# Taking GpSimd out of a chunked recurrence: scaling, masks and clearing on VectorE, -v as one product, decoding behind the last solve

## The chip, the cores and the metric

The kernel runs on one core of one Trainium2 chip. The metric is the device time of one execution in microseconds (us). An engine's instructions run in the order in which the program holds them; the five engines and the DMA queue of SyncE (SP) wait for each other through semaphores.

## The reference

Three layers follow each other on float32 data.

```python
# 1: delta rule, B=4, H=8 (32 heads), S=768 tokens, D=48
k_n = k / (norm(k) + 1e-6)
for t in range(S):
    y[:, :, t] = q[t] @ state                      # state: 48x48 per head
    v_old = state^T @ k_n[t]
    state = state + beta[t] * outer(k_n[t], v[t] - v_old)
# 2: soft mixture of 8 experts with 4 slots each over x = y (3072 tokens x 384)
logits = x @ phi                                   # 32 slots
slot_in = softmax over tokens (logits).T @ x
slot_out = relu(slot_in @ w1) @ w2                 # expert by expert, 384 -> 1024 -> 384
x = softmax over slots (logits) @ slot_out
# 3: gated feed-forward, 384 -> 2048 -> 384
h = x @ w_in;  out = (h * sigmoid(1.702 h)) @ w_out
```

`w_in` and `w_out` arrive as float64 and are turned to float32 on the chip by integer operations ("decoding").

## The kernel before

**Recurrence.** The 768 tokens are cut into 24 steps of 32 (`NS`, index i); four steps make a group (`GS`, 6 groups, index gq). Within a step the delta rule is a triangular system of 32x32 per head. For each step `grams` multiplies k with k and k with q; ScalarE copies the results out of PSUM, and the k-q part (`pm`) is masked to its triangle (L491), by GpSimd in steps 16 to 23 (`PMX`) and by VectorE in the others. For each group `solve` inverts the triangular systems of all its steps on VectorE: a transpose (L499), a clearing of the result `xx` by ScalarE (`clear`, L392), norms of k by small steps, 31 elimination steps of a product (L531) and an addition (L535) each, and a transpose back (L539, called `nt`).

A step itself is `chain(i, g)`, for two halves g: V puts -v into a PSUM bank by a product with the negated identity (L571), KS adds k times state onto it (L578), four pieces of 32 partitions are copied out as `rbd` (three by ScalarE, L589, and one by VectorE, L591, which subtracts v itself instead of taking V's help), U multiplies with the inverse (L604), the result is copied to `ubd` (L614), S adds to the state in PSUM (L622), which ScalarE copies out as `sbd` (L633) for the next step, and QS (L598) and Y (L644) give the output. v has been scaled by the norm of k before (`scale_v`, L740, on GpSimd), as soon as its load has landed. `logits` follows with transposes (T, L657) and the running softmax over tokens.

**Order.** All of this up to the dispatch of tokens to slots is not issued as written. `Plan` collects the operations with an engine, a duration from the kernel's own cost function and their dependencies, works out start times by list scheduling and then by passes from the latest times back and forward again, and issues everything in the order of these times. It knows five engines and SP's queue; a weight load counts 4.4 us (`WD`) there, a load of v 0.6 us plus 2.0 until its data can be used, plus 0.28 us from one engine to another. Where it sees TensorE idle for long, `fill` puts in small products on a zero tile (L383), as many as its own times leave room for. `DBONUS` lowers the rank of decoding in the first of these passes.

**Weights.** SP loads four blocks of `w_in` into slots during the recurrence, `win_decode` turns them to float32 on VectorE in 16 pieces of three passes (L242, L243, L244). Blocks of `w1` and `w2` (8 each, 1.5 MB) go to wherever the recurrence leaves room: two slots early, four `wb` buffers, the ring `cs` of the last three steps (`tail_in`), and the slots that decoding frees (L752).

**Behind the plan** everything is written out by hand: the experts (`expert_in`, `hidden_t`, `expert_out`), which load the rest of `w2` and then `w_out` as blocks come free, the products of `w_in` with the slots, and the final loop over 96 blocks, in which VectorE decodes `w_out` and GpSimd splits it (L1040).

## Time and profile before

| what | value |
|---|---|
| median of 3 runs | 529.67 us (528.14 to 534.84) |
| the profiled execution, its own time | 530.09 us |
| its span, first to last instruction | 528.4 us |
| busy: TensorE, VectorE, ScalarE, GpSimd | 496.1, 344.1, 326.9, 70.8 us |
| mean granted TensorE clock | 0.987 of full speed |
| GpSimd: scalings of v; masks | 24, 22.0 us; 8, 6.3 us |
| moved by DMA | 76.45 MB |

Busy times are sums over a profiled execution whose span is a little shorter than its time. Where products run beside each other in different columns of TensorE, its busy time counts the stretch once. A row of a timeline gives start, duration, engine, line, operation, the tile written and those read, how many instructions are merged in it, and in brackets how long the engine was idle before and what released it. A row of groups gives busy time, mean duration and the idle time before.

### The profile page before, as it was taken

How to read it: one execution, taken by the hardware profiler on the slowest of the kernel's cores; microseconds unless marked ns; L12 is line 12 of the kernel's file. 1: busy time of each engine (PE TensorE's matmuls, PEld its weight loads, DVE VectorE, ACT ScalarE, POOL GpSimd, SP SyncE). 2: the span in 40 equal slices, each digit the busy share in tenths (PEclk: the TensorE clock that was granted, in tenths of full speed). 3: DMA queues.
4: the chain of work that ended last, by engine and by line, in shares of the span. 5: the costliest groups of instructions: out<-in, count | busy, mean ns of one | idle time of the engine just before them, and what ended most of it. 6: DMA issues, size and time to landing. Idle time of an engine off the chain costs nothing.

```text
span 528.4 us, 17593 instructions
## 1 busy us (share of the span) xinstructions
PE 496.1 (94%) x7414; PEld 416.8 (79%) x7414; DVE 344.1 (65%) x910; ACT 326.9 (62%) x736; POOL 70.8 (13%) x113
## 2 busy tenths in 40 slices
PE   7679998999989989999899999999999999999997
PEld 6559776667667667667554898899999999999997
DVE  4989899799998998978653699732333333323322
ACT  8492688778888889787331654644544544545442
POOL 5100011121112011420511333200000000000000
PEclk9798999999999999999989999999999999999999
DMA  8776559666786674687999400100100100100101
GB/s 170 202 195 177 122 158 284 165 174 192 277 285 218 229 249 132 212 297 255 386 419 424 195 0 2 60 1 1 60 1 0 62 1 0 61 0 4 57 2 60
DMA packets 27631, 76.45 MB, mean 145 GB/s; under 512 B 3424, under 2 KB 12640, under 8 KB 24608
## 3 DMA queue, kind: packets, MB, share of 16 engines
q1 hardware_dynamic: 27552, 75.33, 43.8%
q8 instruction: 58, 0.95, 0.8%
q14 instruction: 21, 0.17, 0.1%
HBM read 70.60 MB, written 4.72 MB: 143 GB/s over the span
## 4 chain that ended last, share of the span: by engine, by line
PE 67%; ACT 13%; DVE 10%; DMA 4%; issue 4%; SPq 1%; POOL 0%; DVEq 0%; ACTq 0%; POOLq 0%
PE ps_s L1082 13%; PE ps_g L1082 7%; PE ps_y L1082 7%; PE ps_t L1082 6%; PE ps_s L622 5%; PE ps_x L604 4%; ACT rbd L589 3%; DMA wa<-in_kq_dram 3%; PE ps_x L1044 3%; PE ps_y L598 2%; PE ps_y L644 2%; ACT sbd L633 2%; PE ps_t L383 2%; PE ps_s L955 2%; ACT ubd L614 2%
## 5 line engine op out<-in xcount | busy, mean ns | idle before, releaser
L1049 DVE TENSOR_TENSOR glo<-wa,ghi 128x512 fp32r<-128x512 f32 x96 | 66.4, 691 | 125.3 <-ACT wa L1048 125.3
L1082 PE MATMUL ps_s<-wo,ghi 128*128 128x384 f32 x300 | 81.3, 336 | 0.0
L1047 ACT ACTIVATE ghi<-ps_x 128x512 fp32r<-128x512 f32 x64 | 38.3, 598 | 60.1 <-PE ps_x L1044 59.3
L531 DVE TENSOR_TENSOR wb<-wb,wb 128x87 f32<-128x87 f32 (+25 forms) x211 | 70.0, 346 | 2.3
L535 DVE TENSOR_TENSOR wb<-wb,wb 128x87 f32<-128x87 f32 (+25 forms) x211 | 68.4, 338 | 2.3
L1082 PEld LDWEIGHTS ps_s<-wo,ghi 128*128 128x128 f32 x300 | 54.8, 188 | 2.0
L633 ACT COPY sbd<-ps_s 48x384 f32<-48x384 f32 x92 | 43.4, 473 | 11.7 <-PE ps_s L622 10.0
L1082 PE MATMUL ps_g<-wo,ghi 128*128 128x384 f32 x150 | 50.3, 335 | 0.0
L1082 PE MATMUL ps_y<-wo,ghi 128*128 128x384 f32 x150 | 50.3, 335 | 0.0
L589 ACT COPY rbd<-ps_x 32x192 f32<-32x192 f32 x138 | 42.7, 310 | 6.7 <-PE ps_x L578 3.8
L740 POOL TENSOR_TENSOR cs<-cs,nr 128x384 f32<-128x384 f32 x24 | 22.0, 920 | 176.3 <-DMA cs<-in_vt_dram 104.8
L1082 PE MATMUL ps_s<-wo,glo 128*128 128x384 f32 x150 | 40.6, 335 | 0.0
L598 PE MATMUL ps_y<-sbd,cs 112*32 112x96 f32 x736 | 37.4, 251 | 3.1 <-issue 2.7
L1082 PE MATMUL ps_t<-wo,ghi 128*128 128x384 f32 x120 | 40.2, 335 | 0.0
L466 PE MATMUL ps_g<-wa 112*32 112x64 f32 x896 | 32.6, 225 | 7.5 <-issue 5.1
L1047 ACT ACTIVATE ghi<-ps_y 128x512 fp32r<-128x512 f32 x32 | 19.2, 599 | 31.0 <-PE ps_y L1044 30.7
L1048 ACT ACTIVATE wa<-ps_x 128x512 f32<-128x512 f32 x64 | 38.0, 594 | 0.0
L578 PE MATMUL ps_x<-sbd,cs 112*32 112x96 f32 x736 | 32.5, 249 | 0.3 <-ACT sbd L633 0.2
L466 PEld LDWEIGHTS ps_g<-wa 112*32 112x32 f32 x896 | 23.3, 111 | 10.6 <-issue 7.3
L383 PEld LDWEIGHTS <-warm 128*128 128x128 bf16 x520 | 26.4, 105 | 4.5 <-issue 1.7
L1082 PEld LDWEIGHTS ps_y<-wo,ghi 128*128 128x128 f32 x150 | 28.2, 188 | 0.7
L1082 PEld LDWEIGHTS ps_g<-wo,ghi 128*128 128x128 f32 x150 | 28.2, 188 | 0.7
(297 smaller groups left out, 1073.8 us busy)
## 6 DMA issues: line engine op xcount, KB each, us to landing
cs<-in_kq_dram SPq DMA_DIRECT2D x48, 224.0 KB, 3.6
wa<-in_w_dram SPq DMA_DIRECT2D x7, 1536.0 KB, 8.9
wb<-in_w_dram SPq DMA_DIRECT2D x6, 1536.0 KB, 8.6
wa<-in_kq_dram SPq DMA_DIRECT2D x42, 192.0 KB, 4.4
cs<-in_vt_dram SPq DMA_DIRECT2D x24, 192.0 KB, 3.6
cs<-in_w_dram SPq DMA_DIRECT2D x3, 1536.0 KB, 8.7
cs<-in_wout_dram SPq DMA_DIRECT2D x3, 1536.0 KB, 15.2
out_dram<-wa SPq DMA_DIRECT2D x24, 192.0 KB, 1.9
```

The costliest lines, as they stand in the source:

```text
L383: nc.tensor.matmul(ps[bank][:, 416:512], warm, warm[:, 0:96], start=True, stop=True)
L466: nc.tensor.matmul(pg[32 * n : 32 * n + 32, z, 2 * m : 2 * m + 2], kds[a][0:112, 4 * j + c], kqd[a][0:112, z, :, 4 * j + c], start=True, s ...
L531: engs[e].tensor_tensor(tmp, xx[:, lo:top, j : j + 1].to_broadcast([P, n, m]), gu[:, j : j + 1, j + 1 :].to_broadcast([P, n, m]), op=ALU.mult)
L535: engs[e].tensor_tensor(xx[:, lo:top, j + 1 :], xx[:, lo:top, j + 1 :], tmp, op=ALU.add)
L578: nc.tensor.matmul(pr[32 * j : 32 * j + 32, c - 2 * g].rearrange("p h e -> p (h e)"), kci[0:112, 4 * j + c], sbd[0:112, j, c].rearrange("p ...
L589: n = nc.scalar.copy(rbd[q, 2 * g : 2 * g + 2, :, j], pr[q])
L598: nc.tensor.matmul(py[32 * j : 32 * j + 32, c].rearrange("p h e -> p (h e)"), qci[0:112, 4 * j + c], sbd[0:112, j, c].rearrange("p h e -> ...
L633: apart(sbs, e, copy[e](sbn[r, :, 2 * g : 2 * g + 2, h], ps_s[g][r]))
L1047: nc.scalar.activation(ghis[k % 3], phs[k % 3], AF.Gelu_apprx_sigmoid)
L1048: nc.scalar.activation(ggs[k % 3], phs[k % 3], AF.Gelu_apprx_sigmoid)
L1049: nc.vector.tensor_tensor(glos[k % 3], ggs[k % 3], ghis[k % 3], op=ALU.subtract)
L1082: nc.tensor.matmul(po[f][:, 0:DM], l_[:, 128 * f : 128 * f + 128], w_out(fc, r), start=(fc == 0 and l_ is ghi and r == 0), stop=False)
```

## The change

GpSimd's scaling of v, its masks and ScalarE's clearing of `xx` for groups 2 to 5 go to VectorE. -v is one product with the whole negated identity for all four pieces, and VectorE's piece of `rbd` becomes a plain copy. ScalarE's cost function has 0.1 us of fixed part in place of 0.052, and V counts 0.33 in place of 0.054. Steps 18 and 19 have both `ubd` copies of a half on ScalarE. `win_decode` is called at the end, depends on the last solve's transpose, and loses its lowered rank. Of the weights, `w1` blocks 2 and 3 go into the ring of steps 21 and 22, `w2` block 0 into that of step 23, and `w2` blocks 1 and 2 into the slots behind decoding; the tables of who lies where (`w2t`, `rawt`) follow.

```diff
--- before.py
+++ after.py
@@ -34,14 +34,13 @@
 FREE = 12
 NA, NBS = 4, 4
 SPLIT = (((0, "dve", 0, 6), (1, "dve", 6, 32)), ((0, "dve", 0, 32),))
-DBONUS = -10.0
 GH = 32
 PAD = 1.0
-PMX = range(16, 24)
+PMX = ()
 
 COPY = (
     (0, ("dve", "act", "act", "act"), ("act", "act"), ("act", "act")),
-    (18, ("dve", "act", "act", "act"), ("dve", "act"), ("act", "act")),
+    (20, ("dve", "act", "act", "act"), ("dve", "act"), ("act", "act")),
 )
 DP = 384
 FBANK = "t"
@@ -399,7 +398,7 @@
             clear(ubds[n].rearrange("p a b c d -> p (a b c d)"), 1536, [("ubd", n, c) for c in range(4)])
 
     def cost(eng, n):
-        return {"dve": (n + 62) / 960.0, "act": 0.052 + n / 1200.0, "pool": 0.15 + 0.00166 * n, "padd": 0.15 + 0.0021 * n}[eng]
+        return {"dve": (n + 62) / 960.0, "act": 0.1 + n / 1200.0, "pool": 0.15 + 0.00166 * n, "padd": 0.15 + 0.0021 * n}[eng]
 
     def dma(dst, src, key, d=0.6):
         pl.add("sp", d, lambda: nc.sync.dma_start(dst, src), (), key if isinstance(key, list) else [key], after=2.0)
@@ -498,7 +497,10 @@
         gk, xk, mk = ("gu", z), ("xx", z), ("sm", z)
         pl.add("dve", 2.0, lambda: nc.vector.transpose(gu, nt.rearrange("p a c h t -> p t (a c h)")),
                [("gs", gq % 4, st) for st in range(GS)], [gk, (gk, 1)])
-        clear(xx.rearrange("p a b -> p (a b)"), 1024, [xk])
+        if gq < 2:
+            clear(xx.rearrange("p a b -> p (a b)"), 1024, [xk])
+        else:
+            pl.add("dve", 0.6, lambda: nc.vector.memset(xx, 0.0), (), [xk])
         diag = gu.rearrange("p a b -> p (a b)")[:, :: C + 1]
         small = lambda f, rd, wr, d=0.105: pl.add("dve", d, f, rd, wr)
 
@@ -536,7 +538,7 @@
 
                 pl.add(e, cost(e, n * m), f1, [gk if j < GH else (gk, 1), xk, (xk, z_)], [("tmp", z, z_, j % 2)], nm=f"sv{gq}")
                 pl.add(e, cost("padd" if e == "pool" else e, n * m), f2, [("tmp", z, z_, j % 2), xk], [(xk, z_)], nm=f"sv{gq}")
-        pl.add("dve", 2.0, lambda: nc.vector.transpose(nt.rearrange("p a c h t -> p t (a c h)"), xx.rearrange("p s t -> p t s")),
+        pl.first["nt", gq] = pl.add("dve", 2.0, lambda: nc.vector.transpose(nt.rearrange("p a c h t -> p t (a c h)"), xx.rearrange("p s t -> p t s")),
                [(xk, 0), (xk, 1), xk], [("gs", gq % 4, st) for st in range(GS)], nm=f"nt{gq}")
 
     def two(i):
@@ -564,20 +566,16 @@
         pr = px[:, 0:192].rearrange("p (c h e) -> p c h e", c=2, h=2)
 
         zero = i == 0
-        qa = [j for j in range(4) if rq[j] == "act" and not zero]
 
         def f():
-            for j in qa:
-                nc.tensor.matmul(px[32 * j : 32 * j + 32, 0:192], negi[:, 32 * j : 32 * j + 32],
-                                 vs[i % VB][:, 4 * g : 4 * g + 4].rearrange("p a e -> p (a e)"), start=True, stop=False)
-        if qa:
-            pl.add("pe", 0.054, f, [("v", i % VB)], [kx], nm=f"V{g}.{i}", cols=192 * len(qa))
+            nc.tensor.matmul(px[:, 0:192], negi, vs[i % VB][:, 4 * g : 4 * g + 4].rearrange("p a e -> p (a e)"), start=True, stop=False)
+        if not zero:
+            pl.add("pe", 0.33, f, [("v", i % VB)], [kx], nm=f"V{g}.{i}", cols=768)
         for c in cs if not zero else ():
             def f(c=c):
                 for j in range(4):
                     nc.tensor.matmul(pr[32 * j : 32 * j + 32, c - 2 * g].rearrange("p h e -> p (h e)"), kci[0:112, 4 * j + c],
-                                     sbd[0:112, j, c].rearrange("p h e -> p (h e)"), start=j not in qa,
-                                     stop=j not in qa or c == cs[1])
+                                     sbd[0:112, j, c].rearrange("p h e -> p (h e)"), start=False, stop=(c == cs[1]))
             pl.first["KS", i] = pl.add("pe", 0.24, f, [("kc", i % VB)] + ksb, [kx], nm=f"KS{g}.{i}", cols=420)
         made = []
         for j in range(4):
@@ -588,7 +586,7 @@
                 elif rq[j] == "act":
                     n = nc.scalar.copy(rbd[q, 2 * g : 2 * g + 2, :, j], pr[q])
                 else:
-                    n = nc.vector.tensor_tensor(rbd[q, 2 * g : 2 * g + 2, :, j], pr[q], vi[q, 2 * g : 2 * g + 2], op=ALU.subtract)
+                    n = nc.vector.tensor_copy(rbd[q, 2 * g : 2 * g + 2, :, j], pr[q])
                 if not zero:
                     apart(made, rq[j], n)
             pl.add(rq[j], cost(rq[j], 192), f, [("v", i % VB)] + [kx] * (not zero), [("rbd", g, j)], nm=f"R{g}.{i}")
@@ -736,8 +734,8 @@
     def scale_v(i):
         gq, st = divmod(i, GS)
         v_, nr = vs[i % VB], nrs[gq % 4]
-        pl.add("pool", cost("pool", 384),
-               lambda: nc.gpsimd.tensor_tensor(v_, v_, nr[:, 8 * st : 8 * st + 8].unsqueeze(2).to_broadcast([P, 8, D]), op=ALU.mult),
+        pl.add("dve", cost("dve", 384),
+               lambda: nc.vector.tensor_tensor(v_, v_, nr[:, 8 * st : 8 * st + 8].unsqueeze(2).to_broadcast([P, 8, D]), op=ALU.mult),
                [("nr", gq % 4)], [("v", i % VB)], nm=f"vs{i}")
 
     def solves(i):
@@ -767,14 +765,11 @@
             w = wis[n][:, lo : lo + DP].bitcast(U32)
             key, first = ("wa", NA + n // 2), n == 0 and m == 0
             to = dtmp if first else w
-            k0 = len(pl.ops)
             for s_ in range(3):
                 pl.add("dve", (DP * (1 + (s_ > 0)) + 130) / 1920.0, lambda f=decode(nc, to, raw, to)[s_]: f(), [("wa", PW[n])],
-                       [("dt", n, m)] if s_ == 1 or first else [("dt", n, m), key], nm=f"dc{n}")
+                       [("dt", n, m)] if s_ == 1 or first else [("dt", n, m), key], nm=f"dc{n}", deps=[pl.first["nt", NG - 1]])
             if first:
                 pl.add("dve", (DP + 130) / 1920.0, lambda w=w: nc.vector.tensor_copy(w, dtmp), [("dt", n, m)], [key], nm=f"dc{n}")
-            for k in range(k0, len(pl.ops)):
-                pl.bonus[k] = DBONUS
 
     def slots_in():
         for n in range(2, 4):
@@ -782,11 +777,6 @@
         for n in range(2):
             w1t.append(slots[2 + n])
             weight(slots[2 + n], w1[n], ("wa", 2 + n), nm=f"w1{n}")
-        for n in range(2):
-            win_decode(2 + n)
-        for n in range(2):
-            w1t.append(slots[n])
-            weight(slots[n], w1[2 + n], ("wa", n), nm=f"w1{2 + n}")
 
     def tail_in():
 
@@ -796,14 +786,21 @@
             [k for k in pl.wr if k in (("xx", 0), ("gu", 1), (("gu", 1), 1)) or k[0] == ("xx", 0) or k[0:2] == ("tmp", 1)],
             [k for k in pl.wr if k[0] in ("sm", "tmp", ("xx", 1)) or k in ("bu", ("xx", 1))],
         )
+
+        for n in range(4):
+            win_decode(n)
+        for n in range(2):
+            w1t.append(css[(NS - VB + n) % VB])
         for n in range(NBS):
             w1t.append(wbs[n])
             pl.add("sp", WD, lambda n=n: nc.sync.dma_start(wbs[n], w1[4 + n]), (), held[n], nm=f"w1{4 + n}")
 
         for n in range(VB):
             s_ = NS - VB + n
-            pl.add("sp", WD, lambda s_=s_, n=n: nc.sync.dma_start(css[s_ % VB], w2[n]), (),
+            pl.add("sp", WD, lambda s_=s_, n=n: nc.sync.dma_start(css[s_ % VB], w1[2 + n] if n < 2 else w2[0]), (),
                    [(m, s_ % VB) for m in ("kc", "qc", "v", "k")] + [("pm", i) for i in range(NS // 2, NS) if i % VB == s_ % VB], after=2.0, nm=f"wc{n}")
+        for n in range(2):
+            weight(slots[n], w2[1 + n], ("wa", n), nm=f"w2{1 + n}")
 
     def setup_loads():
         pl.add("sp", 0.5, lambda: nc.sync.dma_start(bu_sb, bu), (), ["bu"], after=2.0)
@@ -844,9 +841,6 @@
             grams(n, [pl.first["KS" if i else "U", i]])
         if i in EXTI:
             win_load(EXTI.index(i), [len(pl.ops) - 1])
-        if i == EXTI[-1]:
-            win_decode(0)
-            win_decode(1)
         if i + LEAD < NS:
             solves(i + LEAD)
 
@@ -872,8 +866,8 @@
     tp = tc.alloc_tile_pool(name="tp", bufs=1, reuse_waits="tile")
 
 
-    w2t = [css[(NS - VB + n) % VB] for n in range(VB)] + [w1t[n] for n in W2P]
-    rawt = [raws[1]] + [cras[(NS - VB + n) % VB] for n in range(VB)]
+    w2t = [css[(NS - 1) % VB], slots[0], slots[1]] + [w1t[n] for n in W2P]
+    rawt = [cras[(NS - 2) % VB], cras[(NS - 1) % VB], raws[0], raws[1]]
 
     def raw_in(n):
         w = 768 if n == 0 else 3072
```

## Rows read from the trace of the kernel before

**Rows 1.** Busy time by stage: window, length, each engine (count), clock, DMA, GB/s.
```profile
54.00:218.50 164.50, 152.85 (x3704) 111.42 (x3707) 150.14 (x454) 137.78 (x351) 23.99 (x27) 1.00 0.67 204
...
259.00:297.00 38.00, 35.06 (x486) 21.23 (x478) 18.09 (x48) 12.55 (x28) 5.80 (x7) 0.96 0.99 410
```

**Rows 2.** The chain of waits, 54 to 218.5 us: shares by line; longest pieces.
```profile
by line: PE ps_s L622 13.7%; PE ps_x L604 9.3%; ACT rbd L589 8.9%; ACT sbd L633 7.4%; ACT ubd L614 5.9%; PE ps_y L598 5.8%; issue 5.3%; PE ps_y L644 5.3%; ACT wb L614 4.8%; PE ps_x L578 4.5%; PE ps_x L571 4.3%; DVE wb L531 4.2%; DVE wb L535
697 pieces in order of time: start us, us, what
...
83.56 1.05 ACT wb L392
...
168.57 1.02 DVE wb L531
```

**Rows 3.** Timeline around two scalings: start, us, engine, line, operation, tiles, shape.
```profile
60.47 0.93 DVE L531 TENSOR_TENSOR wb<-wb,wb 128x252 f32<-128x252 f32 x1
...
211.36 0.32 DVE L531 TENSOR_TENSOR wb<-wb,wb 128x156 f32<-128x156 f32 x1
...
211.41 0.96 POOL L740 TENSOR_TENSOR cs<-cs,nr 128x384 f32<-128x384 f32 x1 [5.84 <-DVE wb L535]
...
211.72 0.83 DVE L535 TENSOR_TENSOR wb<-wb,wb 128x156 f32<-128x156 f32 x1
```

**Rows 4.** Groups by line, GpSimd: busy, mean ns, idle before and what ended it.
```profile
L740 POOL TENSOR_TENSOR cs<-cs,nr 128x384 f32<-128x384 f32 x24 | 22.0, 920 | 176.3 <-DMA cs<-in_vt_dram 104.8 <-DVE wb L531 19.6 <-DVE nr L523 19.3
```

**Rows 5.** The instructions that read v's tensor: from issue to landing, 24 loads.
```profile
DMA to landing us min/median/max: 2.5/3.6/8.6
```

**Rows 6.** Groups by line, VectorE, for prices (L591 of 54 to 218.5 us).
```profile
L243 DVE SCALAR_TENSOR_TENSOR we<-wa,we 128x384 uint32<-128x384 uint32 x8 | 4.4, 554 | 0.2
...
L491 DVE TENSOR_TENSOR wa<-wa,mask 128x256 f32<-128x256 f32 x8 | 3.3, 415 | 0.0
...
L349 DVE COPY wa<-zeros 64x512 f32<-64x512 f32 x4 | 2.3, 639 | 0.0
...
L242 DVE TENSOR_SCALAR we<-we 128x384 uint32<-128x384 uint32 x7 | 2.5, 353 | 0.0
...
L591 DVE TENSOR_TENSOR rbd<-ps_x,cs 32x192 f32<-32x192 f32 x38 | 12.9, 341 | 9.1 <-PE ps_x L578 3.4 <-PE ps_g L466 2.7 <-ACT xt L660 1.2
...
L614 DVE COPY ubd<-ps_x 32x384 f32<-32x384 f32 x10 | 5.5, 549 | 4.3 <-PE ps_x L604 4.2
```

**Rows 7.** Groups by line, ScalarE (L392 has four of 1024 behind 50 us).
```profile
L614 ACT COPY ubd<-ps_x 32x384 f32<-32x384 f32 x46 | 21.6, 470 | 9.2 <-PE ps_x L604 6.9 <-issue 1.4 <-ACT xt L660 0.3
...
L392 ACT COPY wb<-zeros 128x1024 f32<-128x1024 f32 (+1 forms) x7 | 7.8, 1108 | 7.0 <-DVE gs L539 7.0
```

**Rows 8.** Timeline of TensorE, 198 to 199.5 us: transposes, then V products.
```profile
198.44 0.55 PE L657 MATMUL ps_t<-ident,x 128*128 128x128 f32 x3
198.92 0.36 PE L571 MATMUL ps_x<-cs,negi 128*32 128x192 f32 x3
...
199.27 0.34 PE L571 MATMUL ps_x<-cs,negi 128*32 128x192 f32 x3
```

**Rows 9.** Fillers (chain), solve 0's transpose, U of step 0; last transpose, first decode.
```profile
44.17 9.80 PE ps_t L383 x228
...
49.82 1.99 DVE L539 STREAM_TRANSPOSE gs<-wb 128x1024 f32<-128x1024 f32 x1
...
53.90 0.84 PE L604 MATMUL ps_x<-rbd,gs 128*32 128x192 f32 x8
...
216.42 2.04 DVE L539 STREAM_TRANSPOSE gs<-wb 128x1024 f32<-128x1024 f32 x1
...
219.34 0.98 DVE L242 TENSOR_SCALAR dtmp<-we 128x384 uint32<-128x384 uint32 x1
```

**Rows 10.** Timeline behind the plan: product of w1 block 3, first decode of w_out.
```profile
264.89 1.84 PE L928 MATMUL ps_y<-wa,sit 128*32 128x256 f32 x24 [2.00 <-DMA wa<-in_w_dram]
...
284.90 0.36 DVE L242 TENSOR_SCALAR wa<-wa 128x384 uint32<-128x384 uint32 x1 [5.98 <-DMA wa<-in_wout_dram]
```

## The prediction

> **What bounds the kernel now.** I read first the busy time by stage, to see where an edit can matter [rows 1]. The recurrence proper, from the first U product at 54 us to the end of the last solve at 218.5, keeps three engines nearly full: of 164.5 us TensorE is busy 152.9, VectorE 150.1, ScalarE 137.8, GpSimd 24.0. VectorE has 14.4 us to spare. From 259 to 297 the DMA engines are at 0.99 of their time and 410 GB/s. Every GpSimd instruction that the change removes lies before 234 us; the final stage keeps its own.
>
> Second, the chain of waits over that stretch [rows 2]. The reader should see that no engine holds it: S, U, Y, KS and QS products alternate with ScalarE's copies, and VectorE's solve (L531) has 4.2%, the V product (L571) 4.3%. Summed over its 697 pieces VectorE has 19.2 us of the chain's 164.5, ScalarE 51.4, TensorE 83.6. One clearing copy on ScalarE stands in it whole, 1.05 us.
>
> Third, VectorE's order of time beside GpSimd's [rows 3, 4]. A solve step of 128x156 takes 0.32 us, and the next one of that shape takes 0.83, because a GpSimd scaling starts inside the step before it. From the one at 60.47 us to the one at 211.72 there are 22 such VectorE instructions, on average 0.46 us longer than their shape takes alone: 22 x 0.46 = 10.1 us of VectorE's busy time is waiting for GpSimd.
>
> Fourth, the two places where a later stage waits: the fillers ahead of step 0 [rows 9] and the expert product that waits for a load [rows 10].
>
> **The change part by part.** The sum is made against the profiled execution: span 528.4 us, 530.09 in all, 0.4 above the median of 529.67. "In the stretch" is 54 to 218.5 us.
>
> *VectorE's balance in the stretch.* Removed: 10.1 us of waiting, since no GpSimd work is left there. Added: 19 of the 24 scalings of v at 0.55 us (the two-input 128x384 row [rows 6]) = +10.5; eight masks at 0.415 = +3.3; four clearings of 1024 elements. No row has a memset of that size on VectorE. A copy of zeros with 512 elements takes 0.64, so 1.28 by doubling; a one-input pass over 384 takes 0.353, so 0.94 by proportion. I take 1.1, between them and next to ScalarE's 1.05 for the same fill [rows 7]: +4.4 (3.8 to 5.1). Removed again: steps 18 and 19 give their four ubd copies back to ScalarE, 4 x 0.55 = -2.2. The rbd piece that becomes a plain copy from PSUM stays near its 0.34: PSUM reads 32x192 elements either way. Balance: -10.1 + 10.5 + 3.3 + 4.4 - 2.2 = +5.9 us on an engine with 14.4 idle, 9.1 of it in front of rbd pieces that wait for KS [rows 6]. It costs +5.9 if the solve sets the pace all along, 0 if the idle time takes it. The chain is the nearer row: 19.2 of VectorE's 150.1 busy us were on it, 13%, so +0.8.
>
> *ScalarE.* Four clearings leave, 4 x 1.05 = -4.2; four ubd copies come, 4 x 0.47 = +1.9 [rows 7]. Net -2.3, and 51.4 of its 137.8 us were on the chain: -0.9 (-4.2 to +1.9). The clearings do not show elsewhere: the solve that reads them comes later on VectorE itself.
>
> *-V as one product.* The three 32-column products per half step run beside each other: two groups of them start at 198.92 and the next V at 199.27, so 0.35 us [rows 8]. Whole-width, two passes of 0.17 remain, plus what a change of shape costs. The transposes, whole-width between narrow products, show that: three of them hold the engine from 198.44 to 198.92, 0.48 us, while inside such a group the starts are 0.11 apart, so about 0.15 goes to the change. That makes 0.49 for 0.35: +0.14 x 46 = +6.4. V's part of the chain, 4.3% of 164.5 = 7.1, is about half of its 38 x 0.35 in the stretch, so I take half: +3.2. Bounds: 0, if V runs while KS waits for sbd, and +6.4. A gain isn't excluded, since 276 issued pieces become 92: -1.0. The Trainium skill, "TensorEngine Tiling (Array Packing)", Key Properties, says that a change of tiling mode drains TensorE; it speaks against this edit, and by it both sides of each V would pay, which makes this term its upper bound; without it the term is nil. The rows of the transposes side with the page.
>
> *Start.* U of step 0 starts at 53.90, but the solve ends at 51.81: between them TensorE still works off 228 fillers, 9.8 us, which the planner counts from its own times [rows 9]. It now sees three scalings more on VectorE ahead of that solve (0.465 us each by the kernel's own cost function), so it may order up to 1.4 us more fillers; on the chip those scalings (1.7) replace as much waiting for GpSimd. Half: +0.7 (0 to 1.4).
>
> *Later decoding.* In the trace the first decode starts at 219.34, after the last solve's transpose ends at 218.46 [rows 9]: the new dependency orders what already was so. Its 48 passes still lie between dispatch's small VectorE steps, so nothing: 0.
>
> *Moved loads.* w1 block 3 was loaded into the slot that decode 3 frees: its product starts at 264.89, after TensorE waited 2.00 us [rows 10]. It and block 2 now go into the rings that steps 21 and 22 leave, where w2 loads stood before; w2 blocks 1 and 2 take the late slots, and are read only in the second half of the expert stage. On SP's queue the waits keep their places: behind the one on decode 3 stand only the expert stage's loads. POOL's constants had a scaling ahead of them and now have none; dispatch is their only reader. That wait goes: -2.0. Next late is the w_out load, for which VectorE then idles 5.98 us; the DMA engines are full up to it, so its landing won't come forward, which bounds the gain between 0 and -2.0.
>
> Sum: +0.8 - 0.9 + 3.2 + 0.7 + 0 - 2.0 = +1.8, so 530.1 + 1.8 = **532 us**. The terms' own ends, added up, are 521 and 544.
>
> **Rivals.** *The lock was what held the pace.* Each GpSimd operation delays not one solve step but also the rbd and ubd copies queued behind it on VectorE, which the chain books under ScalarE and TensorE. For it: a lengthened solve step of 1.02 us is among the chain's longest pieces [rows 2], and the orders of VectorE were written without these waits. Then the 10.1 us leave the path, the added work goes into the 14.4 idle, ScalarE gives its 2.3 and the load its 2.0, V costs nothing: 530.1 - 10.1 - 2.3 - 2.0 + 0.7 = 516. Against it: the added work is longer than the wait removed.
>
> *VectorE now waits for v's load.* On GpSimd the scaling waited for its DMA at no cost: 104.8 us idle for that [rows 4]. On VectorE everything behind it waits too: solve steps, rbd pieces, then U. The planner counts 0.6 + 2.0 + 0.28 = 2.9 us from issue to use; the trace has a median of 3.6 and a worst of 8.6 [rows 5]. A scaling placed just when the planner thinks it lands stalls VectorE 0.7 us, the worst 5.7: 20 x 0.7 + 5.7 = 19.7 at most. It decides when more than half of that is met: +10 over the forecast, 542. Against it: v is loaded more than a step ahead of its use, and a planner that works back from late times with a full VectorE need not place it at the landing.
>
> *It does not do what it says.* If the planner sets the scalings into waits that VectorE has anyway, if V hides, and if the decode was late already, only the load remains: 528, inside the forecast's band.
>
> **How the numbers follow.** About 2%, 10.6 us, is what a measurement of this kernel can tell from no change: 519.1 to 540.3. Forecast, with the third rival in it: 0.58. The first rival: 0.24, and the second: 0.18; each is past 2%. Both are kept that high since every term of the forecast is a small difference of large ones and the planner reorders the whole recurrence. The forecast's own range is 523 to 539. Eight in ten: I reach down to 517 and up to 542, which leaves out about half of the first rival and under half of the second.
>
> **What would show it.** VectorE's solve steps should all keep their lone duration; the page's GpSimd count should fall by 32 instructions. VectorE's busy time in the recurrence should grow by about 6 us. A wait of VectorE for the v load in the list of waits shows the second rival; the interval between last-solve ends, below 32 us, the first. V products should show two pieces per half step, with about half a microsecond to the next line. The product on w1 block 3 should start with no wait for a DMA, and the final stage (297 to 528) keep its length. I am wrong if the recurrence, 54 to 218.5, changes by more than 8 us.

## The result, and the profile after

The kernel after takes 534.21 us (median of 20 runs, 531.41 to 540.47), the kernel before 528.09 beside it (20 runs, 526.47 to 534.84). The ratio is 1.0105, 95% interval 1.0081 to 1.013: slower by 5.5 us, which is measurable here, yet within 2%. The prediction was 532 and no change past 2%.

The profiled execution of after took 532.09 us (span 530.4), 2.1 below its median; that of before lies 2.0 above the median of its 20 runs. So the two traces differ by 2.0 us where the medians differ by 6.1. Single traces show where time went; the ratios say how much. Two traces that issue the same work in the same order still differ by some 2 us (the kernel before and e5 below, 1.9 at step 20), so a difference of that size between two traces is no finding by itself.

Busy time of after by stage, in the columns of [rows 1].

```profile
54.00:218.50 164.50, 156.07 (x3474) 111.28 (x3472) 149.62 (x477) 132.10 (x341) 0.00 (x0) 1.00 0.64 198
...
259.00:297.00 38.00, 36.55 (x518) 22.30 (x515) 19.18 (x58) 12.62 (x32) 6.50 (x15) 1.00 1.01 419
```

GpSimd is out of the recurrence; its count on the page is 81 for 113. TensorE is busy 3.2 us more in the same window, ScalarE 5.7 less. VectorE stays the same only because the window now holds less of the recurrence, as the next table shows. A window that holds the same steps goes from the first U product of step 0 to that of step 23; before and after:

```profile
53.90:243.90 190.00, 177.75 (x4246) 129.02 (x4246) 171.32 (x501) 157.83 (x404) 32.42 (x55) 1.00 0.68 214
```

```profile
54.00:250.40 196.40, 187.51 (x4075) 132.10 (x4073) 177.32 (x540) 156.90 (x406) 0.00 (x0) 1.00 0.65 205
```

TensorE is busy 9.8 us longer in it and idle 3.4 us less (8.9 for 12.3). The recurrence is longer by TensorE's own time, not by its waits.

Starts of the first U product of a step, of the first expert product and of the first product with `w_in`, read from the traces (us), and the span's end. The last four are experiments told of below. The trace of e6 comes from an execution 4.2 us above that kernel's median, so its row shows the shape and not the size of the loss.

```
                 U0     U4     U8    U12    U16    U20    U23   expert   w_in    span
before          53.9   86.8  122.7  156.4  188.5  219.9  243.9   258.8  294.9   528.4
after           54.0   87.0  124.0  160.2  191.8  223.7  250.4   264.1  297.0   530.4
weights only, old order (e5)
                53.2   86.9  122.8  156.6  190.4  221.8  245.5   260.4  293.1   526.6
e5 + scaling and masks on VectorE (e12)
                54.4   87.3  122.9  156.4  190.1  221.4  245.5   260.4  293.5   527.0
e5 + whole V (e13)
                52.2   86.1  120.8  157.4  190.8  223.6  248.7   263.9  297.7   531.2
late decoding only (e6)
                56.4   91.6  126.6  161.3  196.5  228.0  252.3   267.9  302.6   536.0
```

After loses 3.8 us by step 12, 2.7 more between U20 and U23, and reaches the experts 5.3 late. From there to `w_in` it needs 32.9 for 36.1. The final stage is unchanged, 233.4 for 233.5.

The chain of waits of after, 54 to 218.5 us: shares by line, then two of its longest pieces (start, us, what), beside [rows 2].

```profile
by line: PE ps_s L620 17.0%; PE ps_x L602 12.0%; PE ps_x L571 7.9%; DMA cs<-in_vt_dram 6.1%; PE ps_y L642 5.8%; PE ps_y L596 5.6%; ACT rbd L587 4.9%; PE ps_x L577 4.7%; ACT ubd L612 4.7%; PE ps_g L465 4.1%; ACT sbd L631 3.5%; PE ps_t L655 3
...
74.32 0.91 DVE wb L503
...
85.71 10.02 DMA cs<-in_vt_dram
```

Summed over its pieces up to U of step 20, the chain has TensorE for 112.2 us where before it had 85.6, ScalarE for 27.4 (51.4), VectorE for 15.2 (19.2). The mix is another, the chain 3.7 us longer. V has 13.7 us of it for 7.1, and a load of v is there, which before's chain had not. That load, issued at 85.71 us, stands in SP's queue right behind a `w_in` block issued at 85.20; in before the block comes after the load (85.76 and 85.36). The order of the queue is another, too.

The groups of after's VectorE (count, busy, mean ns, idle before), beside [rows 4, 6], then two of its waits from 54 to 258 us (in total, times, longest).

```profile
L533 DVE TENSOR_TENSOR wb<-wb,wb 128x87 f32<-128x87 f32 (+27 forms) x211 | 63.1, 312 | 2.5
L537 DVE TENSOR_TENSOR wb<-wb,wb 128x87 f32<-128x87 f32 (+27 forms) x211 | 63.1, 312 | 2.0
...
L738 DVE TENSOR_TENSOR cs<-cs,nr 128x384 f32<-128x384 f32 x24 | 13.2, 550 | 3.6 <-DMA cs<-in_vt_dram 3.6
...
L503 DVE MEMSET wb<- 128x1024 f32 x4 | 3.6, 912 | 0.7 <-issue 0.7
```

```profile
DVE rbd L589 <- PE ps_x L577: 4.4, 7, 1.2
DVE cs L738 <- DMA cs<-in_vt_dram: 3.6, 3, 2.2
```

The two solve groups took 70.0 and 68.4 us before (346 and 338 ns): the waiting for GpSimd is gone, 12.2 us of it. A step of 128x252, which took 0.93 us beside a scaling on GpSimd in [rows 3], takes 0.42 in after's timeline of VectorE (start, us). Here it stands behind a scaling that has just waited 2.17 us for its load:

```profile
95.75 0.56 DVE L738 TENSOR_TENSOR cs<-cs,nr 128x384 f32<-128x384 f32 x1 [2.17 <-DMA cs<-in_vt_dram]
...
96.67 0.42 DVE L533 TENSOR_TENSOR wb<-wb,wb 128x252 f32<-128x252 f32 x1
```

TensorE in after, timeline of 201 to 204 us, beside [rows 8]: V is two pieces, and the next line starts 0.42 to 0.52 us later.

```profile
201.50 0.59 PE L571 MATMUL ps_x<-cs,negi 128*128 128x192 f32 x2
202.02 0.87 PE L620 MATMUL ps_s<-ubd,cs 128*48 128x96 f32 x16
...
203.20 0.49 PE L571 MATMUL ps_x<-cs,negi 128*128 128x192 f32 x2
203.62 0.54 PE L577 MATMUL ps_x<-sbd,cs 112*32 112x96 f32 x16
```

The places where later stages wait, from after's timelines, beside [rows 9, 10]: fillers, U of step 0, the last transpose, the first decode, the expert products with the moved blocks, the first decode of `w_out`.

```profile
45.22 8.84 PE L382 MATMUL ps_t<-warm 128*128 128x96 bf16 x204
53.99 0.84 PE L602 MATMUL ps_x<-rbd,gs 128*32 128x192 f32 x8
...
218.59 1.99 DVE L541 STREAM_TRANSPOSE gs<-wb 128x1024 f32<-128x1024 f32 x1
...
220.72 0.34 DVE L241 TENSOR_SCALAR dtmp<-we 128x384 uint32<-128x384 uint32 x1
...
264.10 2.80 PE L922 MATMUL ps_x<-wa,sit 128*32 128x256 f32 x48
266.72 2.77 PE L922 MATMUL ps_y<-cs,sit 128*32 128x256 f32 x48
...
290.19 0.36 DVE L241 TENSOR_SCALAR wa<-cs 128x384 uint32<-128x384 uint32 x1 [9.51 <-DMA cs<-in_wout_dram]
```

The product on the moved blocks starts with no wait, and `w_out` is what is late next.

### The profile page after: what moved, and what is told of

It is laid out like the page before. It is cut to its first block, busy times and chain, and to the rows that moved or that the text cites. A ratio compares the mean times of both kernels' runs of the same rounds, so it can differ in the third digit from the quotient of the medians.

```text
span 530.4 us, 17214 instructions
## 1 busy us (share of the span) xinstructions
PE 502.7 (95%) x7238; PEld 418.1 (79%) x7238; DVE 344.5 (65%) x942; ACT 324.8 (61%) x736; POOL 38.3 (7%) x81
## 4 chain that ended last, share of the span: by engine, by line
PE 73%; DVE 10%; ACT 9%; DMA 4%; issue 3%; POOL 0%; SPq 0%; DVEq 0%; ACTq 0%
PE ps_s L1076 12%; PE ps_s L620 7%; PE ps_y L1076 6%; PE ps_t L1076 6%; PE ps_g L1076 6%; PE ps_x L602 5%; PE ps_x L571 3%; DVE wa L242 3%; PE ps_y L642 3%; PE ps_y L596 3%; PE ps_x L1038 2%; PE ps_x L577 2%; PE ps_t L382 2%; PE ps_s L949 2%; DMA wa<-in_kq_dram 2%
## 5 line engine op out<-in xcount | busy, mean ns | idle before, releaser
L533 DVE TENSOR_TENSOR wb<-wb,wb 128x87 f32<-128x87 f32 (+27 forms) x211 | 63.1, 312 | 2.5
L537 DVE TENSOR_TENSOR wb<-wb,wb 128x87 f32<-128x87 f32 (+27 forms) x211 | 63.1, 312 | 2.0
L1041 ACT ACTIVATE ghi<-ps_y 128x512 fp32r<-128x512 f32 x32 | 19.2, 599 | 31.0 <-PE ps_y L1038 30.7
L465 PE MATMUL ps_g<-wa 112*32 112x64 f32 x896 | 30.6, 225 | 5.2 <-issue 3.3
L596 PE MATMUL ps_y<-sbd,cs 112*32 112x96 f32 x736 | 31.0, 250 | 0.5 <-issue 0.3
L382 PE MATMUL ps_t<-warm 128*128 128x96 bf16 x480 | 29.1, 220 | 2.2 <-ACT ee L691 1.2
L612 ACT COPY ubd<-ps_x 32x384 f32<-32x384 f32 x48 | 22.5, 470 | 10.4 <-PE ps_x L602 9.0
L465 PEld LDWEIGHTS ps_g<-wa 112*32 112x32 f32 x896 | 22.1, 111 | 8.2 <-issue 4.2
```

Of the source, the lines that this page charges most:

```text
L382: nc.tensor.matmul(ps[bank][:, 416:512], warm, warm[:, 0:96], start=True, stop=True)
L465: nc.tensor.matmul(pg[32 * n : 32 * n + 32, z, 2 * m : 2 * m + 2], kds[a][0:112, 4 * j + c], kqd[a][0:112, z, :, 4 * j + c], start=True, s ...
L533: engs[e].tensor_tensor(tmp, xx[:, lo:top, j : j + 1].to_broadcast([P, n, m]), gu[:, j : j + 1, j + 1 :].to_broadcast([P, n, m]), op=ALU.mult)
L537: engs[e].tensor_tensor(xx[:, lo:top, j + 1 :], xx[:, lo:top, j + 1 :], tmp, op=ALU.add)
L596: nc.tensor.matmul(py[32 * j : 32 * j + 32, c].rearrange("p h e -> p (h e)"), qci[0:112, 4 * j + c], sbd[0:112, j, c].rearrange("p h e -> ...
L1041: nc.scalar.activation(ghis[k % 3], phs[k % 3], AF.Gelu_apprx_sigmoid)
```

## The experiments

Ratios are to the kernel before, run on the same chip, with their 95% intervals.

**e1: narrow V in after's order.**

```diff
-            nc.tensor.matmul(px[:, 0:192], negi, vs[i % VB][:, 4 * g : 4 * g + 4]..., start=True, stop=False)
+            for j in range(4):
+                nc.tensor.matmul(px[32 * j : 32 * j + 32, 0:192], negi[:, 32 * j : 32 * j + 32],
+                                 vs[i % VB][:, 4 * g : 4 * g + 4]..., start=True, stop=False)
```

> The changed kernel with -v as four products of 32 columns each, in the same place of the same plan: order and dependencies of all engines are the changed kernel's, only the shape of V differs. If V's whole width is the loss (theory A: 0.14 us more per V on TensorE, half of 46 on the chain, plus the shape changes), it takes 3 to 6 us less than the changed kernel: ratio to before 0.999 to 1.005, and a pair of V's holds TensorE about 0.35 us each in place of 0.49. If VectorE's load or the planner's order is the loss (theories B and C), it stays at the changed kernel's 1.0105, within 0.003.

1.0097 (1.0062 to 1.0132): nothing came back that can be measured. The trace, of the slowest execution but one, shows time lost and time won. From step 0 to step 6 it falls 6.4 us further behind after's: TensorE pauses for 1.97 and 2.39 us in the middle of a group of products, for no cause that the profile shows, and behind each pause the granted clock is at half, as it is nowhere in after's recurrence:

```profile
86.00:89.40 3.40, 3.40 (x70) 2.50 (x60) 3.26 (x11) 1.41 (x4) 0.00 (x0) 0.51 0.52 148
96.40:103.10 6.70, 6.24 (x65) 3.91 (x65) 2.50 (x6) 2.36 (x5) 0.00 (x0) 0.50 0.26 66
```

From step 6 to the last half step it wins 3.5 us back, 1.6 of them from step 17 on. So the ratio says that a narrow V gains nothing in this order; whether the pauses belong to it or only to this execution is not shown.

**e2: scaling back on GpSimd**, everything else as after.

```diff
-        pl.add("dve", cost("dve", 384),
-               lambda: nc.vector.tensor_tensor(v_, v_, nr..., op=ALU.mult),
+        pl.add("pool", cost("pool", 384),
+               lambda: nc.gpsimd.tensor_tensor(v_, v_, nr..., op=ALU.mult),
```

> The changed kernel with the scaling of v back on GpSimd, all else as changed. If VectorE's waits for v's load and its added load are the loss (theory B: 3.6 us of DMA waits in the trace, 10 us of that load on the chain), it takes 4 to 8 us less than the changed kernel: ratio 0.995 to 1.003. If GpSimd's blocking of solve steps costs as much as the scaling itself (0.46 against 0.55 us each), it stays within 2 us of the changed kernel: ratio 1.007 to 1.014. Theory A expects the latter.

1.0062 (1.0029 to 1.0095): below after's 1.0105, with intervals that just overlap. VectorE no longer waits for a load of v. The second rival is worth some 0.4% by this (between 0 and 0.8 by the intervals), and this kernel was ordered anew as well, so that the order may be what differs.

**e3: weights and decoding alone.** Before, with the changed calls of `win_decode`, its dependency and the new places of the weights; all engines as before (no diff beyond those parts of the change).

> The kernel before with only the new places of the weights and the decoding behind the last solve. From the removed wait for w1 block 3: 2 us less, up to 4 us if the experts also start the later loads earlier: ratio 0.992 to 0.997. If the DMA engines, full from 259 to 297 us, only move the wait: 1.000 within 0.002. Theory C (the planner's order shifts with any edit): anything between 0.99 and 1.01, with the difference already there before 250 us.

1.0071 (1.0043 to 1.0098). Slower, though the first four expert products take 12.6 us for 16.4. U of step 20 is at 223.5 for 219.9 (221.8 in e5 below, the same weights in before's order): the recurrence pays. Its work is the same but for a few fillers (16 more in the whole kernel); its order is not.

**e4: V undone in after**: three narrow products, VectorE subtracting v, V's cost 0.054 again, planned anew.

> The changed kernel with V as before in all respects: narrow products only for ScalarE's pieces, 0.054 us in the plan, and VectorE's piece subtracting v itself. Theory A: like the run with four narrow products, ratio 0.999 to 1.005. Theory C: it differs from that run by 3 us or more either way, since the plan's cost of V and with it the order of the recurrence differ.

1.0106 (1.0067 to 1.0145), as after. With the first experiment: undoing V's width alone does not make after faster.

**e5: weights alone, in before's order.** The same loads in the same places of the queue; only what they load differs.

```diff
-            w1t.append(slots[n])
-            weight(slots[n], w1[2 + n], ("wa", n), nm=f"w1{2 + n}")
+            w1t.append(css[(NS - VB + n) % VB])
+            weight(slots[n], w2[1 + n], ("wa", n), nm=f"w1{2 + n}")
...
-            ... nc.sync.dma_start(css[s_ % VB], w2[n]) ...
+            ... nc.sync.dma_start(css[s_ % VB], w1[2 + n] if n < 2 else w2[0]) ...
```

> The kernel before with every operation of its plan in its place, only the contents of five loads exchanged: w1 blocks 2 and 3 go where w2 blocks 0 and 1 went, w2 blocks 1 and 2 behind decoding. If the placing of the weights is a gain and the order of the recurrence is what the run with weights only lost by (theory C), the recurrence ends as before and the experts take 2 to 4 us less: ratio 0.992 to 0.997. If the loads themselves cost the recurrence (a rival: DMA traffic next to it), it loses as the run with weights only did: ratio 1.004 to 1.010.

0.9949 (0.9915 to 0.9983). This beats both kernels. Its two first expert products follow each other, and the wait of 9.31 us for `w_out` comes after:

```profile
260.43 2.80 PE L928 MATMUL ps_x<-wa,sit 128*32 128x256 f32 x48
263.04 2.77 PE L928 MATMUL ps_y<-cs,sit 128*32 128x256 f32 x48
...
286.31 0.36 DVE L242 TENSOR_SCALAR wa<-cs 128x384 uint32<-128x384 uint32 x1 [9.31 <-DMA cs<-in_wout_dram]
```

**e6: later decoding alone**: before, with the dependency on the last transpose, the late call and no lowered rank; weights where they were.

```diff
-                       [("dt", n, m)] if s_ == 1 or first else [("dt", n, m), key], nm=f"dc{n}")
+                       [("dt", n, m)] if s_ == 1 or first else [("dt", n, m), key], nm=f"dc{n}", deps=[pl.first["nt", NG - 1]])
```

> The kernel before with decoding made to depend on the last solve's transpose and called late, as in the change; weights where they were. In the trace of before decoding starts behind that transpose anyway, so no engine gets other work: only the planner's order differs. Theory C: the recurrence is 4 to 5 us longer, and the wait for w1 block 3 stays, so ratio 1.008 to 1.016. If the order does not matter: 1.000 within 0.003.

1.0075 (1.0043 to 1.0108). Nothing was given to another engine, and only fillers were added, 16 in the whole kernel. From step 0 to step 23 TensorE is busy 181.2 us for 177.8 in before, and idle 14.7 for 12.3. Some 1.7 us of that (an estimate: half of 3.4) is the clock: at 89.12 TensorE has waited 1.27 us for ScalarE's copy `xt`, and up to 92.5 us the granted clock is at half. e3, ordered alike, has the same wait at 86.27 and the same fall behind it; before has none in the recurrence. Both windows of e6:

```profile
56.40:252.30 195.90, 181.24 (x4243) 130.47 (x4241) 173.01 (x507) 158.92 (x404) 29.29 (x55) 0.99 0.65 206
89.20:92.50 3.30, 3.30 (x40) 2.33 (x41) 2.06 (x7) 1.09 (x3) 0.13 (x1) 0.50 1.07 232
```

VectorE's waits for KS in the recurrence (54 to 260 us) went from

```profile
DVE rbd L591 <- PE ps_x L578: 3.4, 6, 1.7
```

in before to this in the experiment:

```profile
DVE rbd L591 <- PE ps_x L578: 12.4, 14, 2.7
```

These waits go with the new order here, but they do not make a kernel slow by themselves: after is slower and has 4.4 us of them.

**e7: a re-ordering with no purpose**: before, with one figure of the planner changed.

```diff
-    LAT = 0.28
+    LAT = 0.27
```

> The kernel before with the planner's latency between engines at 0.27 us in place of 0.28: the same operations on the same engines, other order. It gauges what a re-ordering by itself does. Theory C, sharpened: before's order is a lucky one, and most others cost some microseconds, so ratio 1.004 to 1.012. If the loss of the two runs with late decoding comes from something specific to decoding, this stays at 1.000 within 0.003.

1.0051 (1.0012 to 1.009). Another order and 20 more fillers, half a percent. VectorE waits 8.3 us for KS, ten times, from 54 to 258 us, and TensorE is busy 179.8 us from step 0 to step 23, 2.1 more than in before, at full clock:

```profile
55.70:247.30 191.60, 179.84 (x4244) 130.36 (x4243) 169.73 (x497) 158.37 (x404) 31.68 (x55) 1.00 0.69 213
```

**e9: scaling on VectorE at GpSimd's places in before's order.** Only the engine that executes it differs.

> The kernel before with the scaling of v issued on VectorE at the places in the order where it stood for GpSimd, which the planner put at the expected landing of v. If VectorE's wait for the load is dear (theory B), most of 21 scalings hold it 0.7 us and more: VectorE waits 8 to 15 us for the load in all, and the time is 5 to 12 us longer, ratio 1.010 to 1.023. If what GpSimd blocked pays for it, the time stays within 3 us: 0.995 to 1.005.

1.0014 (0.9977 to 1.0052). The waits of the second rival are there, in more places than in after, and VectorE has the scalings' own 13 us. The lock of the first rival is mostly gone: the two solve groups take 129.1 us for 138.4, and five of their steps still wait beside the eight masks on GpSimd. The exchange changes nothing measurable; what each side of it is worth alone this run does not say. The waits for v:

```profile
DVE cs L740 <- DMA cs<-in_vt_dram: 6.2, 6, 1.4
```

**e10: the engine edits and the new weights in before's order** (without the `ubd` copies of steps 18 and 19).

> All that the change does to the engines (scaling, masks and clearing on VectorE, V whole-width with VectorE's piece as a copy, the weights' new places), issued in the order of the kernel before: the plan is before's, with its own engines and costs. Theory C (the loss is the order): between the run with exchanged contents and a little above it, ratio 0.994 to 1.002. If the moved work itself is the loss (theories A and B): near the changed kernel, 1.007 to 1.013.

1.0060 (1.0033 to 1.0087): 1.1% above the weights alone (0.9949), and less than after's 1.0105.

**e11: the old engine work in after's order**: scaling and masks on GpSimd, clearing on ScalarE, narrow V, at the places that after's plan gave them.

> The converse: the changed kernel's plan and order, with scaling and masks issued on GpSimd, the clearing on ScalarE, V narrow for ScalarE's pieces and the subtraction on VectorE, as before; weights as changed. Theory C: it stays near the changed kernel, ratio 1.006 to 1.013. Theories A and B: it comes back to 1.000 or below, as far as the moved work was the loss.

1.0189 (1.0145 to 1.0233), the slowest of all. The solve has 8.1% and 8.0% of its chain (56.5 to 228 us), 4.2% before [rows 2]:

```profile
by line: PE ps_s L624 13.2%; PE ps_x L606 9.4%; DVE wb L533 8.1%; DVE wb L537 8.0%; issue 5.7%; PE ps_y L646 5.7%; PE ps_y L600 4.9%; ACT rbd L591 4.8%; PE ps_g L465 4.8%; PE ps_x L580 4.7%; PE ps_x L573 4.3%; ACT ubd L616 4.1%; ACT sbd L63
```

So the new order needs the new engines: the engine edits together are worth 0.8% in the new order and lose 1.1% in the old one. V is among them, so this is not the price of GpSimd's part. From step 0 to step 23 the narrow V keeps TensorE busy 181.5 us here, 6.0 less than after's whole one in the same order; the time is the same 196.4, because TensorE is idle 14.9 us for 8.9:

```profile
56.50:252.90 196.40, 181.52 (x4257) 129.67 (x4259) 171.99 (x497) 160.88 (x409) 30.52 (x55) 1.00 0.64 202
```

**e12: weights, scaling and masks, old order.**

> A version meant to beat both: before's order, contents of five loads exchanged, and scaling and masks on VectorE at GpSimd's places. The exchange gave 0.9949 and the scaling alone 1.0014, so about the exchange's: 0.992 to 0.998. Below 0.992 would say that the blocked solve steps were on the path after all.

0.9971 (0.9941 to 1.0001). Not better than the weights alone. It starts 1.2 us later (U0), and from step 1.5 on each half step's U lies within 0.5 us of theirs, at both signs: scaling and masks are worth nothing measurable either way, here with no solve step left waiting for GpSimd (126.8 us for the two groups, 138.0 in e5).

**e13: whole V alone, with the weights, old order** (V and VectorE's plain copy as in the change).

> The kernel before in its own order, with the changed contents of the five weight loads and, of the engine work, only the edit on -v: one product with the whole negated identity, and VectorE's piece of rbd as a plain copy. The same order with the weights alone measured 0.9949 of the kernel before, with weights, scaling and masks on VectorE 0.9971, with all of the engine edits 1.0060; the 0.9% between the last two belong to the whole V with the copy, or to the four clearings on VectorE. Theory V (whole-width V costs time wherever VectorE's piece does not hide it, some 0.1 us in half of 46 half steps): 1.001 to 1.006, with U of step 20 ending 1 to 3 us later than 221.8 us. Theory C (the four clearings, 0.9 us each, stand in VectorE's queue ahead of the solve in an order written for ScalarE; V costs nothing, as in the new order): 0.993 to 0.997, U of step 20 at 221 to 222 us. Half-way, near 0.999: both share it.

1.0054 (1.0024 to 1.0083), 1.05% above the weights alone. That is nearly all that the engine edits cost in the old order (1.0060 with the scalings, masks and clearings too). The half steps say where. Against the weights alone U is 1.0 us earlier at step 0, 0.6 later at step 18 and 3.6 later at the last half step: 3.0 of the 4.6 us come in the last eleven half steps, 0.27 each. In e10, the other kernel with the whole V in this order, they are 2.2. There TensorE is full. Windows from U20 to U23 (columns as above), the weights alone, then with whole V, then after:

```profile
221.80:245.50 23.70, 23.36 (x518) 16.55 (x518) 18.99 (x45) 18.67 (x51) 9.27 (x28) 1.00 0.78 279
```

```profile
223.60:248.70 25.10, 24.65 (x494) 16.52 (x494) 18.99 (x45) 18.62 (x51) 7.60 (x27) 1.00 0.73 262
```

```profile
223.70:250.40 26.70, 26.24 (x506) 17.33 (x505) 22.80 (x54) 20.14 (x54) 0.00 (x0) 1.00 0.64 231
```

TensorE has 0.3 to 0.5 us idle in each, and the whole V is 1.3 us of its busy time in six half steps. What VectorE and ScalarE do is the same in the first two. In after VectorE has 3.8 us more work in this window, so V is at most a part of what makes it 26.7 us.

Over a longer stretch, from step 0 to step 18 and to step 23, first the weights alone, then with whole V:

```profile
53.20:204.40 151.20, 137.84 (x3367) 100.55 (x3365) 137.14 (x418) 124.61 (x316) 22.72 (x25) 1.00 0.69 211
53.20:245.50 192.30, 178.37 (x4246) 129.42 (x4246) 171.89 (x502) 157.80 (x404) 33.91 (x55) 1.00 0.68 214
```

```profile
52.20:205.00 152.80, 141.80 (x3227) 100.77 (x3225) 137.31 (x418) 124.70 (x316) 22.91 (x25) 1.00 0.68 207
52.20:248.70 196.50, 184.84 (x4066) 129.69 (x4066) 172.97 (x503) 157.87 (x404) 33.28 (x55) 1.00 0.67 208
```

Whole V costs TensorE 4.0 us up to step 18 and 6.5 up to step 23. Up to step 18 TensorE's idle time shrinks by 2.4 us, so 1.6 of the 4.0 reach the time; behind it there is none left to shrink. Of the 2.4, 1.1 are pauses without a shown cause (last section), so not all of it is sure to be V's doing.

## Why the prediction was right, and where its steps failed

The forecast (532, no change past 2%) held; its sum of +1.8 us stands against a measured +5.5. One term was wrong in kind, and others were off in size. That the total came so near is in part luck: the term left out is worth up to 1.2%, V alone reached nearly its upper end, and the two do not add. The ends of the sum, 521 and 544, were added to the span of 528.4; from the 530.1 of the forecast they are 523 and 546.

**Later decoding, "nothing: 0": this step failed.** It was argued from the chip, where decode already started behind the last transpose. That stayed so (220.72 after 218.59 + 1.99). But the dependency, the later call and the lowered rank are also what the planner works back from, and the order of the whole recurrence came out otherwise. Alone that costs 0.75% (e6), and with the weights it turns a gain of 0.5% into a loss of 0.7% (e5, e3): 1.2%, with V one of the two large parts found. Which of the three edits moves the order most was not tried. The prediction had seen that "the planner reorders the whole recurrence", put it into the chances of the rivals, and gave it no term and no rival.

**Moved loads, -2.0.** Right in place and mechanism, low in size: expert start to `w_in` takes 32.9 for 36.1 us, -3.2, and -3.4 in the kernel with the weights alone, whose ratio is -0.5%. The rest is TensorE's clock, which the step left out though [rows 1] had its 0.96. Busy time from the transposes behind that product to the next `w1` product, before and then after (columns as above):

```profile
266.67:269.84 3.17, 3.17 (x20) 3.01 (x16) 2.27 (x6) 0.72 (x2) 0.00 (x0) 0.58 1.01 426
```

```profile
269.42:271.33 1.91, 1.91 (x20) 1.72 (x17) 1.36 (x5) 0.72 (x2) 0.00 (x0) 1.00 0.93 392
```

The same work takes 1.26 us longer before, at a granted clock of 0.58; 2.00 + 1.26 is the gain. The bound at -2.0 was wrong for a second reason: `w_out` is late next for VectorE, 26.1 us behind the first expert product in both kernels, as said, but TensorE's products with `w_in` did not wait for it.

**-V as one product, +3.2 (0 to +6.4).** In before's order +1.05% (e13 against e5), some 5.5 us, and TensorE's busy time grows by 6.5 us, the upper end. In after's order whole V costs TensorE much the same, 6.0 us (e11), but undoing it gives no time back: four narrow products nothing within 0.4% (e1), and e4, planned anew, agrees. The Trainium skill, "TensorEngine Tiling (Array Packing)", Key Properties, has TensorE drain at a change of tiling mode: the 0.42 to 0.52 us to the next line, for 0.35 [rows 8], agree with it, and so do the 0.20 to 0.27 per half step behind step 18 (e10, e13). How much of the price reaches the time it does not say: up to step 18, 1.6 of 4.0 us did.

**VectorE's balance, +5.9 busy, taken +0.8.** Busy between U0 and U20 went from 151.6 to 154.5, +2.9, of which 1.2 is decoding that now falls in front of U20. The 10.1 us of waiting were read rightly for their stretch; the 12.2 above count three steps ahead of 54 us too. But a clearing took 0.912 us, not 1.1, and only five of the eight masks still stand ahead of U20. Scalings (0.55) and masks (0.416) cost what the rows gave. The idle time in front of `rbd` was misread: 3.4 of its 9.1 us end with KS [rows 6]. At the sum's level +0.8 was near enough: e12 puts scaling and masks at nothing measurable.

**ScalarE, -0.9; start, +0.7.** ScalarE left the chain by 24 us without the chain growing shorter, so its relief bought nothing that shows. U0 starts at 53.99 for 53.90, after 204 fillers for 228. The start alone lies between 52.2 and 56.4 us in the table's traces, so no tenths can be read from it.

**The rivals.** The first (the lock held the pace) fell: with 9.3 of its 12.2 us gone (e9) the ratio is 1.0014, and with all of it gone (e12) 0.9971, 0.2% above the weights alone: no gain, where the rival forecast one past 2%. VectorE took the scalings in exchange, 13 us of work, so the exchange is shown to be free and not the lock by itself. The Trainium skill, "SBUF — State Buffer", SBUF: two separate sides, says that GpSimd and a two-input VectorE operation lock each other out for a whole instruction; the traces agree (0.93 us for 0.42). The second (VectorE waits for v) is real and small: three waits, 3.6 us in after, some 0.4% by e2, and in e9 twice as many at no net cost. Its estimate of ten took the planner's 2.9 us for every load; 21 of the 24 scalings of after found their load landed. The third (it does not do what it says) held for the scaling alone.

**What stays open.** The parts do not add: weights -0.5%, order +1.2%, V +1.05% would make +1.8%, and after has +1.05%. Taken in turn, the weights lead to 0.9949, a new order to 1.0071 (e3) and the engine edits to 1.0105; or the weights to 0.9949, the engine edits to 1.0060 (e10) and the new order to 1.0105. That the new order, planned with the whole V in it, makes room for it would fit; it is not shown. Where after's recurrence loses can be told from TensorE: of the 9.8 us that it is busy longer, 6.0 are the whole V (after against e11) and 3.7 the new order (e11 against before), and 3.4 are won back from idle time. Why an order is worse is shown only in part. In e3 and e6 there are the wait of 1.27 us, the fall of the clock behind it and some more fillers; of after's 3.7 us the fillers are about 1.2, and the rest is open. Three orders other than before's were timed with before's engine work (e3, e6, e7), all slower by 0.5 to 0.75%; whether an order as good exists for the new engine work was not tried.

## What to carry to other kernels

In a kernel whose order comes from a planner, each edit of a dependency, a cost or a call is two edits: price the work with the order held fixed, and the order with the work held fixed, before adding them. The same product can be paid for in part out of idle time where its engine has some, and is paid in full where it has none, so a term needs the stage as well as the duration. And a small, certain part (here, which block loads where: -0.5%) is worth shipping alone.

## What the runs showed of the hardware

A wait of 2.00 us on TensorE went with 3.3 us lost. In before the product of [rows 10] waits that long for its load; then the granted clock is 0.50 from 266 to 269 us, the 1.2 GHz level, and groups of four transposes take 1.12, 1.06 and 1.05 us, which take 0.66, 0.61 and 0.60 in after at 1.00.

```profile
266.00:267.00 1.00, 1.00 (x10) 0.33 (x3) 0.00 (x0) 0.21 (x1) 0.00 (x0) 0.50 1.04 430
267.00:268.00 1.00, 1.00 (x6) 1.00 (x5) 0.54 (x2) 0.26 (x1) 0.00 (x0) 0.50 0.96 406
```

e9 shows it again: a wait of 2.12 us for the same load, and the clock at 0.50 from 265 to 267 us. Behind waits of 0.78 us (e7) and 0.61 (e6) for that load it stays at 1.00; behind the wait of 1.27 us in the recurrence of e3 and e6 it falls.

TensorE can also pause inside a group of products with nothing in the profile that it waited for. In before, e5 and e12, at the same product of step 5, the pause is 2.18, 2.21 and 1.89 us; in e9, with the same order and the same work for TensorE, it is 0.26. Its cause is open.

Clearing 128x1024 by a memset on VectorE takes 0.912 us, less than the 1.05 of ScalarE's copy of zeros [rows 2]. Exchanging 9 to 11 us of VectorE's blocked time for 13 us of scalings on VectorE changes nothing measurable (e9, e12), while 0.5 to 1.2 percent hangs on the order of nearly the same instructions.
